# Bank-wise waits on a three-bank score tile, and zero matmuls until the first scores

## The chip, the cores and the metric

The kernel runs on one core of one Trainium2 chip. The metric is the device time of one execution in microseconds (us), as the median over runs. The profile shows one execution; its span is about 2 us shorter than the measured time of the same run. All runs told of here are of the fast state, with a mean granted PE clock between 0.988 and 1.

The engines have short names in the profile: PE is TensorE's matmuls, PEld its weight loads, DVE is VectorE, ACT is ScalarE, POOL is GpSimd, SP issues the transfers.

## The reference

A transformer block on 2048 tokens of width 640: layer norm, attention with 32 heads of 20 columns, output projection, residual, layer norm, a gated MLP of width 1728, residual.

```python
qkv = (x @ wqkv).reshape(B, S, 3, H, Dh) ...            # on layernorm(x)
scores = jnp.einsum("bhqd,bhkd->bhqk", q, k) * (Dh ** -0.5)
p = _softmax(scores, axis=-1)
o = jnp.einsum("bhqk,bhkd->bhqd", p, v)
h = x + o @ wo
g = jnp.einsum("bsd,df->bsf", y, w_gate)                 # y = layernorm(h)
u = jnp.einsum("bsd,df->bsf", y, w_up)
h2 = h + jnp.einsum("bsf,fd->bsd", g * u, w_down)
```

The scores are 32 x 2048 x 2048 numbers: 2048 PSUM banks of 128 x 512. Each needs an exponential, and that is the bulk of the work outside PE.

## The kernel before

The program has no loops on the chip. While the kernel is built, a model of the five engines plays through the work with assumed durations and writes down, for each engine, the order of its instructions. That order is then fixed. Real waits are made afterwards from the data.

Scores come in bursts into two PSUM tiles in turn, A0 with three banks and A1 with two. ACT takes the exponential of a burst in one instruction. Of the 2048 banks, 312 go to DVE instead, which works out the exponential in five steps. Such a bank is either one of two spare banks ("m"), or the third bank of A0.

```python
A = [None, pools[0].tile([P, 2, QW], F32, name="A1", tag="A1")]
A[0] = pools[0].tile([P, 3, QW], F32, name="A0", tag="A0")
...
def s_option(self, t):
    u = self.unit % 2
    if self.a_free[u].t is None:
        return INF, None, 0.0
    size = 3 - u
    banks = self.peek(size)
    ...
# in s_act: the scores, all first pieces before all second pieces
for _, o, l, rh in sorted(todo, key=lambda x: x[0]):
    mm(o, l, rh, True, True)
...
if third is not None:                       # DVE reads A0's third bank
    self.a_free[u] = Max([self.a_free[u], third.free])
```

So in the model, A0 comes free when both its readers are done; and on the chip the next scores wait for both.

The clock granted to PE stands at half at times: in the profile before from 8.62 to 15.45 us and from 22.28 to 25.69 us, each time after a stretch of 3.41 us in which PE was busy for only 40% and 56%. The model puts in matmuls of zeros ("fill") where PE would be idle:

```python
if known([self.zeros]) <= t and sum(w for x, w in self.recent if x > t - TICK) < ENOUGH:
    ...
        if self.att.summing() is not None or self.att.between(t) or any(b.free.t is not None and b.free.t <= t for b in self.mbanks):
            return t + 10.0, self.fill
...
def fill(self, s):
    ...
    self.charge(s, n / 2.4 + 3.0, self.shape(), float(n), deps, [])
```

The softmax here doesn't subtract the row's maximum and nothing guards it: scores larger than these inputs give would overflow.

## Time and profile before

| | before |
|---|---|
| time, median of 4 runs | 864.82 us (864.53 to 865.33) |
| span of the profile | 863.1 us |
| first exponential starts | 17.11 us |
| last exponential ends | 826.45 us |
| exponentials on ACT, banks on ACT, banks on DVE | 729, 1736, 312 |
| of these on the third bank of A0 | 87 |

The lines of the profile stand in the prediction below. Three readings matter. The sliced view tells where an engine is full. The table of windows tells busy microseconds in a stretch. For ACT, neither shows small stalls, because one exponential's record begins before the last one's ends. So the prediction works with start-to-start times out of the trace, and calls what they have above their floors **excess**; the tables below use the word in this sense. Where a stretch is named, an excess is put down to the time at which the exponential before it starts.

### The profile page before, as it was taken

How to read it: one execution, taken by the hardware profiler on the slowest of the kernel's cores; microseconds unless marked ns; L12 is line 12 of the kernel's file. 1: busy time of each engine (PE TensorE's matmuls, PEld its weight loads, DVE VectorE, ACT ScalarE, POOL GpSimd, SP SyncE). 2: the span in 40 equal slices, each digit the busy share in tenths (PEclk: the TensorE clock that was granted, in tenths of full speed). 3: DMA queues.
4: the chain of work that ended last, by engine and by line, in shares of the span. 5: the costliest groups of instructions: out<-in, count | busy, mean ns of one | idle time of the engine just before them, and what ended most of it. 6: DMA issues, size and time to landing. Idle time of an engine off the chain costs nothing.

```text
span 863.1 us, 34690 instructions
## 1 busy us (share of the span) xinstructions
PE 813.7 (94%) x15473; PEld 359.8 (42%) x15473; DVE 752.6 (87%) x1604; ACT 803.4 (93%) x751; POOL 20.6 (2%) x33
## 2 busy tenths in 40 slices
PE   6999999999989899999999999999999999999998
PEld 2444333223424223223344333344444444556676
DVE  5664897999999999998999999998999998889572
ACT  4879999999999999999999999999999999999921
POOL 3020000000000000000000000000000000000000
PEclk8999999999999999999999999999999999999999
DMA  7132311312341343210311223233224431156200
GB/s 212 49 80 55 92 34 51 95 53 90 84 105 52 76 109 71 54 23 22 84 31 28 60 65 72 52 88 93 40 47 94 99 61 29 28 131 124 45 6 24
DMA packets 140490, 58.34 MB, mean 68 GB/s; under 512 B 111028, under 2 KB 138292, under 8 KB 140340
## 3 DMA queue, kind: packets, MB, share of 16 engines
q1 hardware_dynamic: 140340, 56.12, 26.6%
q8 instruction: 121, 1.98, 1.0%
q14 instruction: 29, 0.24, 0.1%
HBM read 45.63 MB, written 8.09 MB: 62 GB/s over the span
## 4 chain that ended last, share of the span: by engine, by line
ACT 56%; PE 31%; DVE 8%; issue 5%; POOL 0%; DMA 0%; ACTq 0%; DVEq 0%; POOLq 0%
ACT E L734 55%; PE m L435 15%; PE A L435 8%; PE acc L435 6%; PE b L435 2%; DVE i L748 2%; DVE ED L781 1%; DVE fr L778 1%; DVE st L992 1%; PE m L1020 0%; DVE hl L775 0%; DVE hh L1456 0%; DVE fr L772 0%; DVE shared L1004 0%; DVE shared L1362 0%
## 5 line engine op out<-in xcount | busy, mean ns | idle before, releaser
L734 ACT ACTIVATE E<-A 128x1536 bf16<-128x1536 f32 (+1 forms) x729 | 794.6, 1226 | 14.9 <-PE A L435 12.3
L435 PE MATMUL A<-qT,kT 32*128 32x256 bf16 (+3 forms) x3001 | 285.3, 297 | 29.6 <-ACT E L734 26.8
L435 PEld LDWEIGHTS <-kT 32*128 32x128 bf16 (+1 forms) x3438 | 96.9, 92 | 248.6 <-issue 221.4
L435 PE MATMUL acc<-E,Vx 128*32 128x256 bf16 (+3 forms) x2820 | 185.2, 302 | 4.9 <-ACT E L734 4.3
L748 DVE TENSOR_SCALAR i<-m 128x512 int16<-128x512 f32 x225 | 153.0, 683 | 14.5 <-PE m L435 13.3
L435 PEld LDWEIGHTS <-Vx 128*32 128x32 bf16 x3328 | 72.5, 95 | 93.7 <-issue 82.6
L778 DVE TENSOR_TENSOR fr<-hl,fr 128x1024 bf16<-128x1024 bf16 (+1 forms) x158 | 106.9, 676 | 1.9
L781 DVE TENSOR_TENSOR ED<-i,fr 128x1024 int16<-128x1024 int16 (+1 forms) x158 | 106.6, 675 | 1.5
L435 PE MATMUL m<-qT,kT 32*128 32x256 bf16 (+2 forms) x327 | 86.7, 315 | 0.0
L435 PE MATMUL m<-Wd,hh 128*32 128x320 bf16 (+1 forms) x1484 | 76.7, 301 | 0.9 <-issue 0.8
L435 PE MATMUL m<-lnT,Wr 128*32 128x512 bf16 (+6 forms) x1200 | 73.8, 346 | 1.6 <-DVE lnT L1029 0.8
L435 PE MATMUL m<-ln2T,wg 128*32 128x512 bf16 (+2 forms) x1020 | 68.1, 348 | 0.6 <-DVE hh L1456 0.2
L775 DVE TENSOR_SCALAR hl<-fr 128x1024 bf16<-128x1024 int16 (+1 forms) x158 | 65.5, 415 | 1.9
L435 PE MATMUL acc<-zt 128*32 128x512 bf16 (+2 forms) x1008 | 66.7, 342 | 0.0
L748 DVE TENSOR_SCALAR i<-A 128x512 int16<-128x512 f32 x87 | 59.4, 683 | 6.4 <-PE A L435 5.4
L772 DVE TENSOR_SCALAR fr<-i 128x1024 int16<-128x1024 int16 (+1 forms) x158 | 63.9, 411 | 0.6
L435 PE MATMUL m<-ln2T,wu 128*32 128x512 bf16 (+2 forms) x940 | 63.4, 349 | 0.1
L435 PEld LDWEIGHTS <-hh 128*32 128x32 bf16 (+2 forms) x1540 | 42.1, 96 | 29.0 <-issue 16.2
L435 PE MATMUL m<-shared,On 128*32 128x320 bf16 (+1 forms) x968 | 46.5, 301 | 0.0
L1456 DVE TENSOR_TENSOR hh<-gs,m 128x512 bf16<-128x512 bf16 (+3 forms) x63 | 34.3, 545 | 7.7 <-PE m L435 6.9
L435 PEld LDWEIGHTS <-Wr 128*32 128x32 bf16 (+1 forms) x1200 | 28.0, 96 | 29.0 <-issue 19.9
L435 PEld LDWEIGHTS <-zt 128*32 128x32 bf16 x1148 | 28.7, 97 | 24.6 <-issue 13.7
(90 smaller groups left out, 536.2 us busy)
## 6 DMA issues: line engine op xcount, KB each, us to landing
wg<-in_B_w_gate_dram SPq DMA_DIRECT2D x47, 160.0 KB
wu<-in_B_w_up_dram SPq DMA_DIRECT2D x47, 160.0 KB
rb<-rd SPq DMA_DIRECT2D x16, 256.0 KB
kT<-kq SPq DMA_DIRECT2D x24, 128.0 KB
kq<-ln2T SPq DMA_DIRECT2D x24, 120.0 KB
out_dram<-ot SPq DMA_DIRECT2D x16, 160.0 KB
shared<-in_A_x_dram SPq DMA_DIRECT2D x14, 160.0 KB
Wd<-in_B_w_down_dram SPq DMA_DIRECT2D x13, 160.0 KB
```

Of the source, the lines that this page charges most:

```text
L435: nc.tensor.matmul(out_, lhsT=lhsT, rhs=rhs, start=start, stop=stop)
L734: apart(readers, nc.scalar.activation(E[:, 0:size, :], src[:, 0:size, :], ACT.Exp, scale=LN2_ / UNIT))
L748: apart(readers, nc.vector.tensor_scalar(it[:, pos, :], bank.ap, BIAS, 0.0, ALU.add, ALU.max))
L772: nc.vector.tensor_scalar(f[:, 0:n, :], it[:, 0:n, :], 127, None, ALU.bitwise_and)
L775: nc.vector.tensor_scalar(h[:, 0:n, :], f[:, 0:n, :], QR, QK, ALU.subtract, ALU.mult)
L778: nc.vector.tensor_tensor(fb[:, 0:n, :], h[:, 0:n, :], f[:, 0:n, :], ALU.mult)
L781: nc.vector.tensor_tensor(e16[:, 0:n, :], it[:, 0:n, :], fb[:, 0:n, :], ALU.add)
L992: es.append(en.add("DVE", dve_ns(HD), [ready[i], st_free[q]], lambda i=i, c=c, s_=s_: nc.vector.bn_stats(s_[:, c, :], srcs[i][:, c * HD:(c ...
L1456: r = en.add("DVE", dve_ns(w), [e, ce, was], lambda: nc.vector.tensor_tensor(hh[0:M, 0:w], gs[0:M, 0:w], ps[0:M, 0:w], ALU.mult), 1)
```

## The change

The intent: scores should wait for each bank by itself, so that two new banks can be written while DVE still reads the third. Where the third bank is still taken, a burst takes two banks instead of waiting. Zero matmuls run without pause until the first scores, so that PE's clock is full when the first projections come. Three smaller parts come with it: all second-stage transposes go through PE instead of a DMA (`TURNP`, with the layer norm at a higher priority), and the two buffers `gs`, which hold the gate until it is multiplied with `u`, are cut in slices where the row block is narrow.

```diff
-TURNP = 4
+TURNP = 0
-LNP = (1.2, 1.2, 1.2, 1.2, 0, 0)
+LNP = (.5, .5, .5, .5, 0, 0, 0)
@@ fill
-            if known([self.zeros]) <= t and sum(w for x, w in self.recent if x > t - TICK) < ENOUGH:
+            if known([self.zeros]) <= t and (self.att.flat == 0 or sum(w for x, w in self.recent if x > t - TICK) < ENOUGH):
-                    if self.att.summing() is not None or self.att.between(t) or any(...):
+                    if self.att.summing() is not None or self.att.between(t) or not self.att.begun or any(...):
@@ waits
+    class Banks:
+        def note(self, inst, banks, write):
+            deps = []
+            for b in banks:
+                if not write:
+                    deps += self.wrote[b]
+                    self.read[b].append(inst)
+                    continue
+                if self.read[b]:
+                    self.before[b], self.read[b], self.wrote[b] = self.read[b], [], []
+                deps += self.before[b]
+                self.wrote[b].append(inst)
+            for d in deps:
+                tc.add_manual_dep(inst.ins, d.ins.name, ...)
+            ...                                # and no other edges between the engines here
@@ planning of bursts
-            size = 3 - u
+            size = 3 if u == 0 and known([self.third]) <= max(t, self.a_free[u].t) else 2
-                        self.a_free[u] = Max([self.a_free[u], third.free])
+                        self.third = third.free
+                if third is None and len(mine) == 3:
+                    self.third = self.a_free[u]
@@ gs
-                gs = T["gs"][gk]
+                gs = T["gs"][gk][:, at * P:at * P + w]
```

Cut here: the bookkeeping of the slices and of the five single banks that the tail uses, and edits without effect (a longer `SPREAD` and `WP`, `range(3, LASTP)`).

## The prediction

> **What bounds the kernel now.** I read the page's sliced view first, to see which engine is full and where. Each digit is the busy share of 1/40 of the span, 21.6 us, in tenths.
>
> ```profile
> PE   6999999999989899999999999999999999999998
> ...
> DVE  5664897999999999998999999998999998889572
> ACT  4879999999999999999999999999999999999921
> ...
> PEclk8999999999999999999999999999999999999999
> ```
>
> ScalarE (ACT) is at 9 from the fourth slice to the last but two, with a weak start and a tail where only PE works. PE and VectorE (DVE) are nearly full too. The table of windows puts numbers to it (columns: PE, PEld, DVE, ACT, POOL busy us, clock, DMA share, GB/s):
>
> ```profile
> 0.00:17.11 17.11, 11.51 (x181) 5.16 (x181) 10.01 (x35) 4.74 (x7) 6.56 (x20) 0.80 0.90 266
> 17.11:60.00 42.89, 38.29 (x792) 16.75 (x791) 27.50 (x78) 35.13 (x32) 7.38 (x4) 0.96 0.19 50
> ...
> 100.00:800.00 700.00, 667.14 (x12495) 278.08 (x12493) 658.49 (x1350) 696.92 (x644) 6.07 (x8) 1.00 0.28 67
> ...
> 826.45:863.14 36.69, 32.55 (x362) 25.60 (x354) 18.39 (x53) 3.71 (x15) 0.55 (x1) 0.98 0.05 15
> ```
>
> In the 700 us of the middle ACT is idle for 3 us only. The groups by form say what it does and how the third bank is used:
>
> ```profile
> L734 ACT ACTIVATE E<-A 128x1024 bf16<-128x1024 f32 x451 | 457.1, 1065 | 8.6 <-PE A L435 7.7 <-PE acc L435 0.4 <-PE m L435 0.2
> L734 ACT ACTIVATE E<-A 128x1536 bf16<-128x1536 f32 x278 | 413.4, 1487 | 6.2 <-PE A L435 4.6 <-PE m L435 0.8 <-DVE On L920 0.3
> ...
> L748 DVE TENSOR_SCALAR i<-A 128x512 int16<-128x512 f32 x87 | 59.4, 683 | 6.4 <-PE A L435 5.4 <-ACT E L734 0.6
> ```
>
> So 729 exponentials work on 451 x 2 + 278 x 3 = 1736 banks, and 87 times DVE reads the third bank of the score tile A0 (225 more times it reads an m bank). Neighbouring ACT records overlap, so their durations overstate the cost. I took start-to-start times from the trace: the tenth percentile is 0.903 us after a two-bank exponential and 1.330 us after a three-bank one. That is 0.427 us a bank and 0.05 us an instruction. Whatever a start-to-start time has above these floors I call **excess**: it is all that better waits could ever give back. It is 32.2 us over the whole stretch of exponentials (17.1 to 826.5 us): about 9 before 60 us, 17.7 between 100 and 800 us, the rest at the two ends. Of the 17.7, 14.6 stands before exponentials of A0, 3.1 before those of A1.
>
> **What the Trainium skill says.** Four places bear on it.
> (1) "TensorE: Matmul & The Clock Gate", Part 1, says that the PE clock is halved after an idle window of about 3.4 us and restored after a busy one. The trace agrees: its clock records show half speed from 8.63 to 15.45 us and from 22.28 to 25.69 us, then full speed to the end.
> (2) "PSUM — Partial Sum Buffer", on bank collisions, says different engines on different banks run clean, and to guard by bank. That makes the new waits legal. The trace has ACT and DVE reading two banks of A0 side by side already.
> (3) "VectorE: DVE Perf Modes", in the table beside the silicon bug, gives ScalarE a fixed part of 172 cycles with a PSUM source. In this stream the trace shows 0.05 us, some 60 cycles of 1.2 GHz, so extra, smaller exponentials are cheap here.
> (4) "DMA: Bandwidth & Descriptors", Alternative transpose paths, names TensorE through PSUM with an identity as the other way to transpose. The trace has both: 13 DMA transposes and, at the start, 16 PE ones.
>
> **Part 1, waits bank by bank.** Before, new scores into A0 waited for ACT and for DVE, wherever each read. I matched all 87 third-bank reads with the exponential of the same burst. DVE starts at the median 0.07 us after ACT and takes 0.68, ACT's two banks take 1.07: so DVE ends **before** ACT, by 0.41 us at the median, and after it in only 11 of 87 cases. The excess of the following A0 exponential is 0.050 us on average after a third-bank read, and 0.044 us after none. The table of waits agrees:
>
> ```profile
> PE A L435 <- ACT E L734: 26.8, 49, 1.3
> ...
> ACT E L734 <- PE A L435: 12.3, 10, 4.7
> PEld L435 <- DVE i L748: 6.9, 20, 0.7
> ```
>
> Waits on DVE stand only before weight loads; DVE holding PE A itself shows 0.6 us in two cases in the tile's view. Sum: the 11 late cases carry 2.6 us of excess; I take half as removed, **-1.3 us**. On the other side, a burst that finds the third bank taken now has two banks; if that adds up to ten exponentials, 10 x 0.05 us is 0.5; I book **+0.3 us**.
>
> **Part 2, zero matmuls until the first scores.** The timeline of PE before the first scores:
>
> ```profile
> 7.82 0.59 PE L1020 MATMUL m<-ident,shared 128*32 128x128 bf16 x24
> 9.69 1.26 PE L1020 MATMUL m<-ident,shared 128*32 128x128 bf16 x40 [1.29 <-DVE shared L1004]
> 11.71 5.03 PE L435 MATMUL m<-lnT,Wr 128*32 128x512 bf16 x56 [0.77 <-DVE lnT L1029]
> 16.68 0.60 PE L435 MATMUL A<-qT,kT 32*128 32x512 bf16 x5
> ```
>
> The last 40 transposes take 1.26 us against 0.82 for the 40 begun at 7.58, and the projections run at half clock until 15.45. K and Q are two groups of five steps of 512 columns. At half clock the trace shows 0.427 us between steps, at full clock half that. Saved before the first scores: about nine cold steps x 0.21 = 1.9, and some 0.4 of transposes. A zero step that stands in the way when data come gives back up to 0.2: **-2.1 us** for the first scores, 16.7 to about 14.6. I expect most of it to reach the end, since the waits up to 60 us (2.4 us at 34.4, 4.7 us at 54.1) are for projections, transposes and DVE, which move along; no transfer ends them. The second cold window, with its 0.8 us gap at 25.2, should go in part: **-0.5 us**.
>
> **Part 3, the second stage transposes on PE.** Gone are 13 DMA transposes, whose landings nothing in the middle waited for. Added are 13 x 20 small matmuls: the 16 tiles at the start cost 7.8 us of PE busy time, so 13 cost 6.3 us, mostly in place of the zero matmuls, which hold PE for over 60 us. DVE gets 13 copies out of PSUM of 0.49 us, 6.4 us, in a middle where it is busy 658 of 700 us. DVE does a bank in 0.68 + (0.41 + 0.42 + 0.68 + 0.68)/2 = 1.78 us. If its whole 6.4 us came out of this, 3.6 banks would move to ACT at 0.43 us, 1.5 us; it has some idle time, so **+0.9 us**.
>
> **Part 4, the tail.** The 36.7 us after the last exponential are PE back to back, with output transfers at the end. With eight slices of gs in place of two buffers for the last 128 rows, the last gate groups need not wait their turn:
>
> ```profile
> 857.60 0.44 PE L435 MATMUL b<-ln2T,kT 128*128 128x128 bf16 x5
> 858.08 0.27 ACT L1443 CAST gs<-b 128x128 bf16<-128x128 f32 x1 [1.54 <-PE b L435]
> 858.38 0.29 DVE L1456 TENSOR_TENSOR hh<-gs,b 128x128 bf16<-128x128 bf16 x1 [1.51 <-ACT gs L1443]
> 858.72 0.55 PE L435 MATMUL b<-Wd,hh 128*128 128x320 bf16 x2 [0.68 <-DVE hh L1456]
> ```
>
> PE idles here from about 858.0 to 858.7 for one late gate; that is worth **-0.7 us**. The bulk stays.
>
> **Sum:** -1.3 + 0.3 - 2.1 - 0.5 + 0.9 - 0.7 = -3.4, so 864.9 becomes **861.5 us**, 0.4% faster.
>
> **Rivals.** *The third bank hides more than I see.* The order of all instructions is fixed when the kernel is built, by a model of durations in which A0 came free only after both readers; it may have placed scores later than needed. For it: 14.6 of 17.7 us excess before A0. Against: A0 holds three banks in most bursts and is refilled during a two-bank exponential of 0.9 us, which makes it tight in any case, and bursts after a third-bank read are no worse. If it holds, some 9 us go: 853 to 856.
> *VectorE becomes the bound.* Its 6.4 us more and the earlier layer norms delay the DVE exponentials, and PE and ACT then wait on them. For it: 94% busy. Against: its share of banks has a cap and priority. That makes 864 to 868.
> *The start's gain is lost* at 54 us to a chain that began earlier, or the zero matmuls get in the way. Then only 0.5 us of part 2 is left: 863 to 864.
>
> **Range and chances.** The parts are small, and a reshuffled order alone can shift the end by 2 or 3 us, so I take 855.5 to 866. Faster by 2% needs 847.6, 17.3 us off. With 32 us of excess, 17 of head and 37 of tail, mostly real work, nearly all the excess would have to vanish: 4%. Slower by 2% needs a new bound: 1%.
>
> **What would show it.** Right: clock full from 5 to 860 us, first exponential at 14.8 to 15.6 us against 17.1; 725 to 745 exponentials; DVE reading 300 to 320 banks; excess from 100 to 800 us between 14 and 18 us; a tail of about 36 us. Wrong: the excess before A0 halves (the first rival), DVE banks fall below 300 or ACT shows waits for DVE's banks (the second), or the first exponential is early but the one at 54 us is not (the third).

## The result

| | before | after |
|---|---|---|
| time, median of 4 runs | 864.82 us | 862.79 us (862.35 to 863.23) |
| span of the profile | 863.1 us | 860.7 us |
| first exponential starts | 17.11 us | 18.94 us |
| last exponential ends | 826.45 us | 827.10 us |
| tail after it | 36.7 us | 33.6 us |
| exponentials, banks on ACT, banks on DVE | 729, 1736, 312 | 738, 1738, 310 |
| excess, whole, and from 100 to 800 us | 32.2, 17.7 us | 29.8, 17.8 us |

The ratio is 0.9976, with a 95% interval of 0.9959 to 0.9993: 0.24% faster. A ratio is the mean time of one kernel's fast runs over the mean of the other's in the same rounds, so it isn't quite the ratio of the medians. In a second sample it was 0.9973.

First the sliced view of after, as in the prediction:

```profile
PE   8899999999989999999989999999999999999998
...
DVE  5664889999989999989989999999999999878663
ACT  3889999999999999999999999999999999999941
...
PEclk9999999999999999999999999999999999999999
```

The clock is full now. But ACT's first slice has fallen from 4 to 3. The windows of after, cut at the same times as before (PE, PEld, DVE, ACT, POOL, clock, DMA share, GB/s):

```profile
0.00:17.11 17.11, 14.77 (x291) 7.48 (x295) 8.47 (x30) 3.91 (x6) 6.55 (x20) 1.00 0.89 264
17.11:60.00 42.89, 38.37 (x826) 16.99 (x818) 28.12 (x83) 35.68 (x34) 7.38 (x4) 1.00 0.17 46
...
100.00:800.00 700.00, 672.44 (x12697) 277.21 (x12697) 660.46 (x1350) 696.75 (x650) 6.98 (x8) 1.00 0.26 64
```

The middle is unchanged: ACT is busy 696.75 us against 696.92, and the excess there is 17.8 us against 17.7. The groups by form of after:

```profile
L761 ACT ACTIVATE E<-A 128x1024 bf16<-128x1024 f32 x474 | 476.1, 1069 | 6.5 <-PE A L435 5.9 <-PE acc L435 0.4
L761 ACT ACTIVATE E<-A 128x1536 bf16<-128x1536 f32 x263 | 391.9, 1490 | 6.1 <-PE A L435 3.2 <-PE m L435 1.4 <-PE acc L435 0.7
```

There are 23 more two-bank exponentials and 15 fewer three-bank ones, and at the very end a single one of one bank. In the table of waits of after (total us, times, longest us) a new line has come up:

```profile
PEld L435 <- ACT E L761: 109.1, 272, 1.3
PE A L435 <- ACT E L761: 22.9, 46, 1.0
...
ACT E L761 <- PE A L435: 9.0, 8, 3.8
```

The bank-wise waits now stand before the weight load of a score, where before they stood before its matmul.

**Where the time went**, from the two traces: the first exponential starts 1.83 us later. Nine more exponentials at 0.05 us and two more banks at 0.427 us are 1.30. The excess is 2.47 us smaller: 2.0 less before 100 us, 0.1 more up to 800, 0.6 less after that. This makes +0.66, and the last exponential does end 0.65 us later. The tail is 3.11 us shorter. The sum is -2.46, and the spans differ by -2.47. The tail of after:

```profile
827.10:860.67 33.57, 29.91 (x333) 23.45 (x332) 16.59 (x47) 3.70 (x14) 0.55 (x1) 0.98 0.05 16
```

These are two single profiles, and not all of this account repeats. Below, b_waits and b_gs have before's order up to the last exponential, a_tile and after_again have after's. The first exponential starts at 17.1, 18.1 and 17.8 us in before, b_waits and b_gs, and at 18.9, 18.2 and 19.2 us in after, a_tile and after_again; the excess is 32.2, 33.3 and 33.6 us against 29.8, 30.5 and 32.2. The tail repeats: 36.7 and 36.6 us in before and b_waits, 33.6 us in all three of after's order. So the gain shows up in the tail, and the part that gives the change its name shows nothing in the middle.

### The profile page after: what moved, and what is told of

Read it like the earlier page. It is cut to its first block, busy times and chain, and to the rows that moved or that the text cites. A ratio compares the mean times of both kernels' runs of the same rounds, so it can differ in the third digit from the quotient of the medians.

```text
span 860.7 us, 35389 instructions
## 1 busy us (share of the span) xinstructions
PE 820.7 (95%) x15853; PEld 360.6 (42%) x15853; DVE 754.4 (88%) x1607; ACT 804.5 (93%) x760; POOL 21.5 (2%) x33
## 5 line engine op out<-in xcount | busy, mean ns | idle before, releaser
L777 DVE TENSOR_SCALAR i<-m 128x512 int16<-128x512 f32 x216 | 147.7, 686 | 15.3 <-PE m L435 13.9
L809 DVE TENSOR_TENSOR fr<-hl,fr 128x1024 bf16<-128x1024 bf16 x156 | 106.3, 681 | 1.9
L812 DVE TENSOR_TENSOR ED<-i,fr 128x1024 int16<-128x1024 int16 x156 | 106.1, 680 | 1.3
L435 PE MATMUL m<-qT,kT 32*128 32x256 bf16 (+3 forms) x319 | 83.4, 313 | 0.0
L806 DVE TENSOR_SCALAR hl<-fr 128x1024 bf16<-128x1024 int16 x156 | 65.1, 417 | 1.5
L803 DVE TENSOR_SCALAR fr<-i 128x1024 int16<-128x1024 int16 x156 | 64.4, 419 | 0.9
L435 PE MATMUL acc<-zt 128*32 128x512 bf16 (+3 forms) x960 | 63.1, 345 | 0.0
L435 PEld LDWEIGHTS <-hh 128*32 128x32 bf16 (+3 forms) x1540 | 42.4, 96 | 27.2 <-issue 15.7
L435 PE MATMUL m<-shared,On 128*32 128x320 bf16 x960 | 46.8, 301 | 0.4 <-DVE shared L1394 0.2
L1482 DVE CAST gs<-m 128x512 bf16<-128x512 f32 (+2 forms) x62 | 34.7, 559 | 8.0 <-PE m L435 7.5
```

The source lines that it names most:

```text
L435: return nc.tensor.matmul(out_, lhsT=lhsT, rhs=rhs, start=start, stop=stop)
L777: r = nc.vector.tensor_scalar(it[:, pos, :], bank.ap, BIAS, 0.0, ALU.add, ALU.max)
L803: nc.vector.tensor_scalar(f[:, 0:n, :], it[:, 0:n, :], 127, None, ALU.bitwise_and)
L806: nc.vector.tensor_scalar(h[:, 0:n, :], f[:, 0:n, :], QR, QK, ALU.subtract, ALU.mult)
L809: nc.vector.tensor_tensor(fb[:, 0:n, :], h[:, 0:n, :], f[:, 0:n, :], ALU.mult)
L812: nc.vector.tensor_tensor(e16[:, 0:n, :], it[:, 0:n, :], fb[:, 0:n, :], ALU.add)
```

## The experiments

Twelve runs were made in three jobs, each on one chip, beside runs of the kernel before on the same chip. All gave correct results. Times differ between chips by 1 or 2 us, so ratios are to before of the same job.

### b_waits: the new waits in the old order

The kernel before with the new waits only. `size = 3 - u` and `Max([...])` stay, so that every instruction stands where it stood.

```diff
-                for _, o, l, rh in sorted(todo, key=lambda x: x[0]):
-                    mm(o, l, rh, True, True)
+                for _, o, l, rh, i in sorted(todo, key=lambda x: x[0]):
+                    r = mm(o, l, rh, True, True)
+                    if i is not None:
+                        guard.note(r, [i], True)
```

Cut here: the class `Banks`, as in the change, and the calls that note the readers.

> The kernel before with only the new waits: scores wait bank by bank, but every instruction stands in the same order as before. Theory 1 (the prediction): only 11 of 87 third-bank reads end after ScalarE, they carry 2.6 us of excess, so the time falls by 0 to 2 us (about 864.8 to 863.5) and the excess before A0 between 100 and 800 us stays at 13 to 15 us. Rival (the third bank hides more): the time falls by 4 us or more and that excess drops below 9 us. Third possibility: the bank waits now sit on the weight loads, so nothing is gained or up to 1 us is lost.

Measured: 866.15 us, before 866.48; ratio 0.9997 (0.9978 to 1.0016). Excess before A0 from 100 to 800 us: 15.0 us; in the old waits and the same order on the same chip (b_gs, below) 14.9. Eleven third-bank reads end after ACT's here too, and the exponentials after them have 2.5 us of excess together, against 2.6 in before: bank-wise waits took nothing off them. The interval of the time alone would leave room for a gain of 1.9 us; the excess shows none. The first rival of the prediction falls.

### a_tile: the old waits in the new order

```diff
         def note(self, inst, banks, write):
-            deps = []
-            ...
+            if write:
+                self.readers = []
+                return
+            for r in self.readers:
+                tc.declare_no_dep(inst.ins, r.ins, reason="they read different banks")
+            self.readers.append(inst)
```

> The kernel after with its order of instructions kept, but with the old waits: the whole three-bank tile at once. If bank-wise waits are worth something on the chip in the new order, this is slower than after (862.8) by 1 us or more, since the new order puts two-bank scores ahead of late third-bank reads. If VectorE is nearly always done first, it is within 0.5 us of after.

Measured: 864.01 us; ratio 0.9969 (0.9954 to 0.9983), where after has 0.9976 and 0.9973. Excess before A0: 14.9 us, in after 14.7. Taking the bank-wise waits out of after costs nothing measurable (the interval is 1.3 us to each side). Of 94 third-bank reads in after, 8 ended later than ACT's read of the same burst, and the exponentials after those 8 have 0.9 us of excess together.

### b_gs: the slices of gs alone

```diff
-                gs = T["gs"][gk]
+                gs = T["gs"][gk][:, at * P:at * P + w]
+                spans = T["gs_free"][gk * TPC + at:gk * TPC + at + nt]
+                gs_was = Max([x[0] for x in spans if x[0] is not None])
```

> The kernel before with only the eight slices of gs for the last 128 rows. Everything up to the last exponential keeps its order. Theory: the tail after the last exponential shrank from 36.7 to 33.6 us because of this part, so the time falls by 2 to 3 us (862 to 863), the last exponential stays at 826.5 us and the gap of 0.7 us before the last Wd matmuls is gone. Rival: the shorter tail comes from what the reordered middle left over for it; then this falls by no more than 0.7 us.

Measured: 865.19 us; ratio 0.9986 (0.9972 to 1.0000). The tail, from the last exponential at 828.53 us:

```profile
828.53:864.38 35.85, 32.47 (x374) 25.70 (x362) 18.37 (x53) 3.70 (x14) 0.55 (x1) 0.99 0.05 16
```

It is 35.85 us, 0.84 less than before's 36.69 (and 0.76 less than in b_waits). So the prediction's step was right in size, and my theory before this run, that the whole 3.1 us come from the slices, was wrong. The rest is in the order. Counted after the last exponential, before has 15 gate and up groups of 5 matmuls with 256 columns at full width; after has 11. Such a group takes 0.55 us in the chain of work that ended last, so four of them are 2.2 us, and 0.8 + 2.2 = 3.0 of the 3.1. The tails of a_tile, a_head and both repeats, which share after's order, are all 33.6 us. The new order did four groups more while ACT was still at work. The count fits other orders too: b_fill, without the slices, leaves 10 groups and a tail of 34.4 us.

### a_head: zero steps charged at their cold cost

The timeline of PE in after shows why the first exponential is late:

```profile
4.68 6.54 PE L435 MATMUL m<-zt 128*32 128x512 bf16 x104
11.05 0.73 PE L1051 MATMUL m<-ident,shared 128*32 128x128 bf16 x40
...
14.25 0.44 PE L1051 MATMUL m<-ident,shared 128*32 128x128 bf16 x17 [0.62 <-issue]
...
15.35 3.22 PE L435 MATMUL m<-lnT,Wr 128*32 128x512 bf16 x56
18.50 0.60 PE L435 MATMUL A<-qT,kT 32*128 32x512 bf16 x5
```

The transposes could have begun at 7.6 us, as they do before. They stand behind 33 zero steps (a step is four matmuls side by side, so 132 of them; before there are 10 steps), and PE takes its matmuls in the order of the program. The model charged 0.216 us a step. The clock was at half until 6.21 us, so the first ten or so took 0.427. All the same, the warm clock pays: from the first projection to the first scores it is 3.15 us here and 4.97 before. The edit only changes what the model charges, so the rest of the order stays.

```diff
-        self.charge(s, n / 2.4 + 3.0, self.shape(), float(n), deps, [])
+        cold = self.att.flat == 0 and s < 8000.0
+        self.charge(s, n / 1.1 if cold else n / 2.4 + 3.0, self.shape(), float(n), deps, [])
```

> The kernel after, but with the model charging 0.465 us instead of 0.216 for a zero step before 8 us, which is what it takes on a cold PE, so that about half as many of them stand before the first transposes. The rest of the order is the same. The first transposes should start near 7.6 us (after: 11.05), the first exponential near 15.0 us (after: 18.94, before: 17.11). Theory A (the start's gain reaches the end): 2 to 3.5 us faster than after, 859.5 to 861. Theory B (it is lost at the wait of 54 us to another chain): the exponential at 54 us comes at 54 us as in both, and the time is within 0.7 us of after.

Measured: 863.24 us; ratio 0.9961 (0.9946 to 0.9976). PE of a_head:

```profile
7.61 0.82 PE L1052 MATMUL m<-ident,shared 128*32 128x128 bf16 x40 [0.84 <-DVE shared L1036]
...
9.77 0.77 PE L1052 MATMUL m<-ident,shared 128*32 128x128 bf16 x40
...
14.47 1.46 PE L436 MATMUL m<-lnT,Wr 128*32 128x512 bf16 x21 [1.12 <-issue]
15.86 0.60 PE L436 MATMUL A<-qT,kT 32*128 32x512 bf16 x5
```

The transposes are in time, and the first exponential starts at 16.30 us. It would have been near 15.2 without 1.12 us in which PE waited for nothing that the profile shows. Beside a_tile, which has the same order from 8 us on and ran on the same chip, every exponential is earlier by the same 1.85 us, from the first to one at 138 us, and by 2.5 us at 700. So the lead isn't lost at 54 us: theory B falls, but the time isn't that of theory A either. It was lost after 805 us: there it is still 2.2 us, and the last exponential ends 1.75 us later than a_tile's. In that stretch PE stood still again and again without a semaphore to wait for (the column in brackets is the idle time just before):

```profile
805.73 0.22 PE L436 MATMUL acc<-E,Vx 128*32 128x128 bf16 x1 [0.75 <-issue]
...
810.85 0.93 PE L436 MATMUL m<-ln2T,qT 128*32 128x256 bf16 x25 [1.16 <-issue]
```

Five such gaps over 0.3 us come to 4.7 us in a_head, against one of 0.65 in a_tile. In the 4 us before each of the five a packet of the instruction queue started, which took 0.88 to 2.70 us; the median packet takes about 1.0. That alone says little, as from 795 to 828 us 84% of all moments have such a packet in the 4 us before them. But the three longest gaps follow the three packets of over 2 us. (In a_best, below, the longest gap, 2.0 us, follows none of that length.)

### after_again and a_head_again: the same two on one chip

> The kernel after itself, on the chip of the next three, so that they are compared on one chip. It should be 0.2 to 0.35% faster than before. Its first exponential should come 1 to 2 us later than before's 17.1 to 18.1 us, and its tail after the last exponential should be 33.6 us, as in the other runs of this order.

> The same kernel as in run a_head, for a second sample beside after. There its lead of 1.85 us lasted to 805 us and was then lost to gaps on PE that no semaphore ends, each after a long packet of the instruction queue. If those gaps are chance, the median is 1.5 to 2.5 us below after_again and the exponential at 800 us comes about 2 us earlier. If they belong to the early order, the time is within 0.7 us of after_again again, with 3 us or more of such gaps between 800 and 830 us.

Measured: after 863.08 us (862.72 to 865.34; ratio 0.9973), a_head 862.77 (858.97 to 865.67; ratio 0.9965, 0.9942 to 0.9987). In the profiled runs a_head's exponentials lead by 3.4 us at the first and by 4.6 us from 32 us to 786 us without a change; 4.06 us are left at the end (spans of 859.3 and 863.4 us). Gaps of the kind above: 2.8 us in a_head, 1.0 in after. So a lead at the start does carry to the last scores, but the medians differ by only 0.3 us: a_head's runs spread over 6.7 us. Whether it is faster than after remains open. The gaps recur in a_head and are fewer, so they are neither pure chance nor fixed.

### a_best: another order of the same work

```diff
-LAT = {"ACT": 170.0, "DVE": 150.0, "POOL": 250.0, "SP": 0.0, "PE": 275.0}
+LAT = {"ACT": 170.0, "DVE": 150.0, "POOL": 250.0, "SP": 0.0, "PE": 274.0}
```

> a_head with one constant of the model changed by 1 ns (the latency of PE, 275 to 274), picked from 26 such orders because it leaves five gate and up groups fewer for the tail (2.7 us of matmuls at full width). If the tail is set by what the order leaves over, it is 30.8 to 31.2 us against 33.6, and the time is 2 to 4 us below a_head's. If such orders do not carry over to the chip, it is within 1 us of a_head's.

Measured: 862.71 us; ratio 0.9965 (0.9953 to 0.9977). The tail is 30.4 us, a little under what was expected. But the last exponential came only at 831.7 us, with 18.5 us of excess before A0 against 15.3 in a_head_again. What the tail gained, the middle gave back, so the 2 to 4 us did not come. With a_head it is the fastest of the kernels by ratio, 0.35% under before, though not resolved from after.

### b_order: a control

The kernel before, with `"PE": 277.0` in the line above and nothing else.

> A control: the kernel before with the same constant changed by 2 ns (275 to 277) and nothing else, so that only the order of instructions is shuffled: 735 exponentials in place of 729 and one gate or up group more in the tail. If shuffling alone can move the time as much as the whole change does, it is 2 to 5 us slower than before. If order does not matter, it is within 1 us.

Measured: 872.65 us; ratio 1.0081 (1.0065 to 1.0097). A change of 2 ns in a planning constant makes the kernel 6.8 us slower. Its last exponential ends at 832.5 us, with 5.5 us more excess than before's profile and 6 exponentials and 3 banks more on ACT. Shuffling alone can cost three times what the whole change gains.

### b_fill: the zero matmuls alone

The two lines of the fill rule in the diff above, on the kernel before.

> The kernel before with only the zero matmuls until the first scores. The prediction's step says first scores 2 us earlier. The trace of after says the zero matmuls stand in the way: first transposes at 11.0 us instead of 7.6 and first exponential at 18 to 19 us, 1 us or more later than before on the same chip, although the clock is full. The time is within 3 us of before, as the whole order is shuffled (735 exponentials).

Measured: 870.07 us; ratio 1.0037 (1.0021 to 1.0054). The first transposes start at 11.15 us and the first exponential at 18.39, so the late start belongs to this part. But by the 135th bank on ACT it is at 89.6 us, before's profile at 88.3. By then the delay is 1.3 us. The rest (the medians differ by 3.75 us, where 3 were allowed) comes later, in an order that is reshuffled as a whole: the excess before A0 is 21.8 us against 14.6. PE's clock is also at half in two more stretches of this profile, 10.2 us together. What is due to which is not shown.

### b_guard: the bank part alone

> The kernel before with only the bank part of the change, waits and planning together: two-bank bursts where the third bank is still taken (742 exponentials in place of 729). If the bank part carries the gain, it is 2 us or more faster than before. If the gain is the tail's, it is no faster: 13 more exponentials are 0.65 us, and its order leaves 1.1 us more of matmuls for the tail, so 0 to 2 us slower.

The edit is that of b_waits with the new planning of bursts. Measured: 873.03 us; ratio 1.0068 (1.0044 to 1.0091), more than the 2 us slower that I allowed for. Its order leaves a tail of 39.7 us. The excess before A0 is 15.9 us, so here, too, the new waits took none away. After 800 us there are 3.7 us more of excess than in before, and in this profile the clock is at half from 797.9 us for 13.65 us.

### a_late and at_late: making VectorE late

If the waits do nothing because DVE is nearly always done first, they should do something once it isn't. Before every sixth third-bank read, DVE gets three idle instructions.

```diff
+                if guarded:
+                    lates[0] += 1
+                    if lates[0] % 6 == 0:
+                        for _ in range(3):
+                            nc.vector.tensor_tensor(idle[:], zt[:], zt[:], ALU.mult)
                 r = nc.vector.tensor_scalar(it[:, pos, :], bank.ap, BIAS, 0.0, ALU.add, ALU.max)
```

> The kernel after with three idle VectorE instructions (1.25 us together) put before every sixth third-bank read, 15 in all, so that these reads end about 0.85 us after ScalarE's read of the same burst. The order is otherwise the same. With bank-wise waits only bursts that need the third bank should wait: about half of the 15. Expected: the exponential after a late read with a two-bank burst has less than 0.2 us of excess, the one with a three-bank burst about 0.6 us; the time 3 to 7 us above after.

> The same 15 late reads with the old whole-tile waits (the order of a_tile). Every next burst of A0 should now wait, two-bank ones too: about 0.6 us of excess in each, and the time 3 to 5 us above that of a_late. If bank-wise waits do nothing even when VectorE is late, the two are equal.

Measured: 876.81 us with bank-wise waits, 878.08 with whole-tile waits (two runs each, and their ranges overlap). The first is 12 to 14 us above after's times on other chips, not 3 to 7 as expected, and the second 1.3 us above it, not 3 to 5. The 15 exponentials after the late reads have 8.2 us of a_late's excess of 45.0, and the rest was not followed up. The traces are clearer. The 15 reads now end 0.95 us after ACT on average. Seven are followed by a three-bank burst: mean excess 0.67 us with the new waits, 0.70 with the old. Eight are followed by a two-bank burst: 0.44 with the new, 0.80 with the old. One of the eight, in the timeline of a_late:

```profile
223.70 0.39 PE L437 MATMUL A<-qT,kT 32*128 32x512 bf16 x2
223.86 0.68 DVE L784 TENSOR_SCALAR i<-A 128x512 int16<-128x512 f32 x1
224.60 0.38 PE L437 MATMUL A<-qT,kT 32*128 32x512 bf16 x1 [0.52 <-DVE i L784]
```

and the same burst in at_late:

```profile
223.71 0.68 DVE L772 TENSOR_SCALAR i<-A 128x512 int16<-128x512 f32 x1
...
224.45 0.39 PE L437 MATMUL A<-qT,kT 32*128 32x512 bf16 x3 [0.90 <-DVE i L772]
```

With the new waits the two banks for ACT are written at once and only the third waits for DVE; the next exponential has no excess, in at_late it has 0.84 us. That is what the change was meant to do. But the wait isn't gone; it has moved on by one exponential. The third bank's matmul holds PE until DVE is done, the scores for A1 stand behind it, and their exponential waits:

```profile
226.02 2.39 ACT L763 ACTIVATE E<-A 128x1024 bf16<-128x1024 f32 x2 [0.67 <-PE m L437]
```

It has 0.80 us of excess here and 0.02 in at_late. Over the six exponentials after this late read the excess is 0.88 us with the new waits and 0.94 with the old.

Only three of the eight have next to no excess at the next exponential (at most 0.04 us). The other five keep 0.47 to 0.88 us. One of them, in a_late:

```profile
464.28 0.28 PE L437 MATMUL A<-qT,kT 32*128 32x256 bf16 x2
464.49 0.68 DVE L784 TENSOR_SCALAR i<-A 128x512 int16<-128x512 f32 x1
465.23 0.39 PE L437 MATMUL A<-qT,kT 32*128 32x256 bf16 x4 [0.67 <-DVE i L784]
465.62 1.02 ACT L763 ACTIVATE E<-A 128x1024 bf16<-128x1024 f32 x1 [0.54 <-PE A L437]
```

Here a bank of scores comes in two pieces of 256 columns, and the scores are sorted by piece: first pieces of banks 0, 1 and 2, then second pieces. The first piece of bank 2 waits for DVE, and the second pieces of banks 0 and 1 stand behind it on PE. So ACT waits for DVE again, by way of PE's order. Of the eight, the two with whole banks of 512 columns escape, but only until the exponential after (the second has 0.92 us over six exponentials, against 0.93 in at_late). A third escapes for good, as its burst writes no third bank at all: 0.44 against 1.29 us. Sorting bank 2's pieces last might make the other five like the first two; it wasn't run, and those two gained under 0.1 us.

Counted so, over six exponentials, 13 of the 15 late reads cost the same with both kinds of waits, within 0.06 us. The others are the one without a third bank and one at 350 us (0.85 against 2.47), where in at_late the clock fell to half at 354.75 us.

## Why the prediction was right

It said 861.5 us and 855.5 to 866; the time is 862.79. The number came out right in part by luck: part 2 was booked at -2.6 us and left after 0.3 us behind, part 1 gave nothing, and the tail gave 2.4 us more than was booked for it.

- **"Part 1, waits bank by bank", -1.3 +0.3.** The reading was right: DVE ends before ACT in nearly all cases, and the waits hide nothing. (The median lead is 0.32 us, as 0.07 + 0.68 - 1.07 gives, and not the 0.41 of the text.) Two swaps of the waits alone (b_waits, a_tile) show no change beyond their intervals, and the eleven late reads kept 2.5 of their 2.6 us, so the -1.3 should have been 0. The extra exponentials were nine, 0.45 us. When DVE is made late on purpose, 13 of 15 late reads cost ACT the same with the new waits, at once or one exponential later; the one saving that the waits explain, 0.85 us, comes where the next burst writes no third bank.
- **"Part 2, zero matmuls until the first scores", -2.1 -0.5.** This step failed: the first exponential came 1.8 us later (about 1 us, if three profiles of each order are taken). The clause that failed is "A zero step that stands in the way when data come gives back up to 0.2": 33 steps stood in the way, 3.5 us. I had priced the warm clock, rightly (the projections up to the first scores take 1.8 us less, where 1.9 was booked), and not the length of the row of zero steps that starts cold. The gap of 0.8 us at 25.2 us did go, and 1.0 us of the wait at 54 us, so that by 59 us after was only 0.3 us behind. a_head shows that with half as many steps the transposes start in time.
- **The third rival, the start's gain lost at 54 us**: no. A lead of 1.85 us in a_head and of 4.6 us in a_head_again passes 54 us whole. The other half of that rival, "the zero matmuls get in the way", is what happened.
- **"Part 3", +0.9.** DVE does 310 banks in place of 312, so two banks moved to ACT, 0.85 us. The number fits, but this part was not run alone, and b_guard and b_order, which leave the transposes as they were, have 310 and 309 banks on DVE too. So its cause is not shown.
- **"Part 4, the tail", -0.7.** The slices alone gave -0.84. What the step missed are four gate and up groups less, 2.2 us: "The bulk stays" was wrong. This is the gain that made up for part 2.
- **The second rival, VectorE the bound**, did not come: DVE is busy 660 us of the middle 700, before 658.

One more reading needs a limit. In its first point on the skill the prediction says that the trace agrees. The times of half clock are there, but what stands before them isn't a stretch of pure idling: in these profiles the clock falls to half 15 times before 850 us, each time after 3.41 us in which PE was busy for 29 to 70%.

The range held because the misses cancelled. Its reason, "a reshuffled order alone can shift the end by 2 or 3 us", was right in kind, but the control shows that this was too small: 6.8 us from 2 ns, which on top of 861.5 lies outside the range. What stays open is what decides whether an order is a good one. The parts of the change are each slower or about equal alone (b_guard 1.0068, b_fill 1.0037, b_gs 0.9986), and together faster, so the result can't be shared out among them, except for the 0.8 us of the slices.

## What to carry to other kernels

Before a wait is removed, match each waiter with its two releasers and see which ends later. Here the wait on VectorE was the earlier one in 76 of 87 cases, and no time came from it. Look as well at what stands behind the waiting instruction on its own engine: in a_late the wait that was taken off one exponential came back at the next. In a kernel whose order is planned by a model, run a control that changes only the order, before any gain of under 1% is put down to a mechanism. A filler that warms a clock runs at the cold rate itself and holds everything behind it on its engine: plan it at that rate, and end it before the data come.

## What the Trainium skill lacked or had wrong

- "Runtime: NRT & Kernel Launch", Instruction fetch mechanics, says that crossing an instruction block costs one step that is mostly hidden. In every run told of here PE has, after 60 us, one to five gaps over 0.3 us, all but one of them after 795 us, where its matmuls follow each other fastest (in before 454 in the 15 us from 800 us, 730 in the 50 us from 100 us), that no semaphore ends: 0.6 us in all in b_fill, 4.7 in a_head. In a_head the three longest followed the three instruction packets of over 2 us, in a_best the longest followed none such. That they are fetch stalls is possible and was not tested.
- "VectorE: DVE Perf Modes", the table beside the silicon bug, gives ScalarE a fixed part of 172 cycles with a PSUM source. It doesn't say what remains of it in a stream. "ScalarE: Activation LUTs", What ACT_TABLE_LOAD costs, does: back-to-back ACTIVATEs overlap by about 93 ns. Here records of 1024 elements overlap the next by 0.14 us at the median, and start to start the runs show 0.903 and 1.330 us for 1024 and 1536 elements, a fixed part of 0.05 us.
- No page says that a wait which is added by hand can end up before a weight load instead of its matmul. Here it did (272 waits, 109.1 us of PEld's time in after). In bursts of A0 where PE had waited, the first matmul came 0.055 us after the end of ACT, against 0.052 in the kernel before, so it cost almost nothing.
